# Two rows a partition of w_out fetched by two GpSimd gathers, and the z projection computed in rows

## The chip, the cores and the metric

The kernel runs on one core of one Trainium2 chip. The metric is the device time of one execution in microseconds (us). Before the change the median of three runs is 126.91 us (126.79 to 127.1). The profiled execution that all the rows below come from took 126.89 us; its span, from the first to the last instruction, is 125.1 us, so 1.8 us lie around it.

## The reference

One token `x` (1 x 576) is normalised and sent down two branches, which are added to it:

```python
xn = _layernorm(x, axis=-1)
return x + _A_ref(xn, k_cache, v_cache, wq, wo) + _B_ref(xn, w_in, w_sp, b_sp, w_out)

# A: attention of one token, 32 query heads on 16 key heads, the last 4096 positions
q = x @ wq                                   # 576 -> 32 heads x 128
scores = einsum('bhqd,bhkd->bhqk', q, k) * 128 ** -0.5
o = einsum('bhqk,bhkd->bhqd', softmax(scores), v)
A = o.reshape(1, 1, 4096) @ wo               # 4096 -> 576

# B: a gated MLP, sequence length 1
z = gelu(x @ w_in)                           # 576 -> 4608
z1, z2 = z[..., :2304], layernorm(z[..., 2304:])
B = (z1 * (w_sp * z2 + b_sp)) @ w_out        # 2304 -> 576
```

All inputs are bfloat16. Keys and values of the window are 16 MB each; with wq, wo, w_in and w_out some 51 MB are read once. There is one token, so every weight is used for one vector.

## The kernel before

The order of the instructions on every engine is written out by hand. All large loads are on one queue, SP's, in the order in which they are consumed: wq, the keys of head group 0 and 1 (four key heads a group, 4 MB each), w_in, keys 2, values 0, keys 3, values 1, 2 and 3, w_out, and wo in five pieces of 14, 9, 6, 2 and 1 rows a partition. They share four SBUF slots (`a` to `d`); a load is issued when the last reader of its slot is done. w_out and wo share two slots (`ends`).

Small vectors come first: x is normalised into `XT` (L206 to L209), the query is computed (L217) and spread into `Qb` (L245). Then come, for each group g and each half c of its positions:

- `keys(g, c)` (L258): VectorE (DVE) transposes the keys, four instructions of 128x1024.
- `scores(g, c)` (L265): TensorE (PE), 16 matmuls into the PSUM tile `S`.
- `sm_a(g)` (L286 to L292): the maximum of the scores on DVE, then four exponentials on ScalarE (ACT).
- `sm_b(g)` (L303, L306): DVE transposes the probabilities, ACT copies them into `PT`.
- `sums`, `pv(g)` (L329): 32 matmuls of the probabilities with the values into `ops`.
- `tail(g)` (L319 to L357): DVE scales and folds `ops`, PE moves it into place (L350), and DVE copies it into `Y`.

Branch B lies between them. `z_mms` (L365) takes x as the moving operand: 162 matmuls, each with 128x128 weights of w_in and two columns, so that z stands in columns (partition p holds 18 elements of each half). It comes on PE after the scores of groups 0 and 1. `z_exp` (L372 to L379) begins on DVE with one copy out of PSUM; it comes after `sm_b(1)` and before `keys(2, 1)`. `z_gelu` and `z_norm` follow later and leave `hv`, 18 columns, one for each row of w_out that a partition holds.

At the end PE adds everything into two accumulators, one for columns 0 to 263 and one for 264 to 575 of the output: `out_hv(0)` and `out_hv(1)` (12 rows of w_out) after `pv(3)`, then the matmuls of `tail(3)`, then `out_hv(2)` (six rows), then 32 rows of wo with `Y` (L465, two matmuls a row). DVE and ACT copy the accumulators out and ACT issues the store.

GpSimd (POOL) makes the identity and masks in the first 8 us, then has only two one-column powers to do (L200, L404).

Of the kernel before, what the change touches and what calls it, by code (L numbers as in the profile page):

```python
# [7 lines left out]

FP32 = mybir.dt.float32
BF16 = mybir.dt.bfloat16  # L10
ALU = mybir.AluOpType
ACT = mybir.ActivationFunctionType
AXX = mybir.AxisListType.X

D = 576
# [12 lines left out]
NF = FH // 128  # L28
CUT = (0, 264, D)
XP = D // 3  # L30
EPS = 1e-5
SCALE = DH ** -0.5
GELU_C = 0.7978845608028654
NS = 9


@with_exitstack
def kernel(
# [14 lines left out]
    nc = tc.nc  # L53
    P = nc.NUM_PARTITIONS
# [5 lines left out]
    work = ctx.enter_context(tc.tile_pool(name="work", bufs=2))  # L60
    ktpool = ctx.enter_context(tc.tile_pool(name="ktpool", bufs=2))
    single = ctx.enter_context(tc.tile_pool(name="single", bufs=1))
    ps_s = ctx.enter_context(tc.tile_pool(name="ps_s", bufs=1, space=bass.MemoryType.PSUM))
    ps_o = ctx.enter_context(tc.tile_pool(name="ps_o", bufs=1, space=bass.MemoryType.PSUM))
    ps_m = ctx.enter_context(tc.tile_pool(name="ps_m", bufs=1, space=bass.MemoryType.PSUM))
    ps_a = ctx.enter_context(tc.tile_pool(name="ps_a", bufs=1, space=bass.MemoryType.PSUM))
# [36 lines left out]
    V[2] = load_kv("b", A_v_cache, 2, "v")  # L103
    V[3] = load_kv("c", A_v_cache, 3, "v")
    ends = [big.tile([P, TP * DH], BF16, name=f"end{n}", tag="ad"[n]) for n in range(2)]
    wout_sb = rows(ends[0], B_w_out, "wout", 0, NF, 0)
    wo_sb = []
    for n, t, at in ((14, 1, 0), (9, 1, 14), (6, 0, NF), (2, 0, NF + 6), (1, 0, NF + 8)):
        wo_sb += rows(ends[t], A_wo, "wo", len(wo_sb), n, at * D)
# [64 lines left out]
    lx = const.tile([P, NG], FP32, name="lx")  # L174
    mb = const.tile([P, 32], FP32, name="mb")
    nc.gpsimd.memset(mb[:], 0.0)

# [32 lines left out]
    nc.tensor.matmul(ps_x[:, 24:26], lhsT=ones_b[:], rhs=spb[:], start=True, stop=True)  # L210
    wb = const.tile([P, 2], FP32, name="wb")
    nc.vector.tensor_copy(wb[:], ps_x[:, 24:26])


    for s, wv in wq_sb:
# [26 lines left out]
    for a in range(4):  # L242
        for h in range(2):
            for k2 in range(2):
                nc.vector.tensor_scalar_mul(qbv[:, a, h, k2], qpv[:, h, k2], mask4[:, a:a + 1])  # L245


    Y = const.tile([P, 32], BF16, name="Y")
    KT = {}
# [2 lines left out]
    def keys(g, c):  # L252

        kT = ktpool.tile([P, TC, 2, 8, GK, 2], BF16, name=f"kT{g}_{c}", tag="kT")
        src = K[g][:, TC * c:TC * (c + 1), :].rearrange("p t d -> p (t d)").bitcast(FP32)
        dst = kT[:].rearrange("p t b r x e -> p (t b r x e)").bitcast(FP32)
        for n in range(4):
            nc.vector.transpose(dst[:, 1024 * n:1024 * (n + 1)], src[:, 1024 * n:1024 * (n + 1)])  # L258
        KT[g, c] = kT

    def scores(g, c):
        kv = KT.pop((g, c))[:].rearrange("p (t s) b r x e -> p b e x t r s", s=2)
        for be in range(4):
            for x in range(GK):
                nc.tensor.matmul(  # L265
                    S[g % 2][32 * x:32 * x + 8, c, :],
                    lhsT=Qb[:, GK * g + x, be].rearrange("p a h -> p (a h)"),
                    rhs=kv[:, be // 2, be % 2, x],
                    start=(be == 0), stop=(be == 3), tile_position=(0, 32 * x),
                )  # L270
# [87 lines left out]


    def z_mms():  # L360
        zps = ps_a.tile([P, 2, NF], FP32, name="zps", tag="a")
        for s, wv in win_sb:
            wt = wv.rearrange("k (p t) -> k t p", t=NF)
            for t in range(NF):
                nc.tensor.matmul(zps[:, :, t], lhsT=wt[:, t, :], rhs=XT[:, s, :],  # L365
                                 start=(s == 0 and t == 0), stop=(s == NS - 1 and t == NF - 1),
                                 skip_group_check=True)
        return zps

    def z_exp(zps):  # L370
        z = const.tile([P, 2, NF], FP32, name="z")
        nc.vector.tensor_copy(z[:], zps[:])  # L372
        u = const.tile([P, 2, NF], FP32, name="u")
        nc.vector.tensor_mul(u[:], z[:], z[:])
        nc.vector.tensor_scalar(out=u[:], in0=u[:], scalar1=0.044715, scalar2=1.0,
                                op0=ALU.mult, op1=ALU.add)
        nc.vector.tensor_mul(u[:], u[:], z[:])
        th = const.tile([P, 2, NF], FP32, name="th")
        nc.scalar.activation(th[:], u[:], ACT.Exp, scale=-2.0 * GELU_C)  # L379
        return z, th  # L380
# [15 lines left out]
    def z_norm(G, sz):  # L396
        psz = ps_m.tile([P, 512], FP32, name="psz", tag="m")
        nc.tensor.matmul(psz[:, 0:2], lhsT=ones_f[:], rhs=sz[:], start=True, stop=True)
        mz = const.tile([P, 4], FP32, name="mz")
        nc.vector.tensor_scalar_mul(mz[:, 0:2], psz[:, 0:2], 1.0 / FH)  # L400
        nc.vector.tensor_mul(mz[:, 2:3], mz[:, 0:1], mz[:, 0:1])
        nc.vector.tensor_sub(mz[:, 2:3], mz[:, 1:2], mz[:, 2:3])
        nc.vector.tensor_scalar_add(mz[:, 2:3], mz[:, 2:3], EPS)  # L403
        nc.gpsimd.tensor_tensor(out=mz[:, 3:4], in0=mz[:, 2:3], in1=mhalf[:], op=ALU.pow)  # L404
        zn = const.tile([P, NF], FP32, name="zn")
        nc.vector.tensor_scalar(out=zn[:], in0=G[:, 1], scalar1=mz[:, 0:1], scalar2=mz[:, 3:4],
                                op0=ALU.subtract, op1=ALU.mult)
# [12 lines left out]
    for g in range(2):  # L420
        for c in range(2):
            keys(g, c)
            scores(g, c)
            if g == 1 and c == 0:
                sm_a(0)
# [27 lines left out]
    tail(1)  # L453
    sm_a(3)
    hv = z_norm(G, sz)
    sums(2)
    pv(2)
    tail(2)
    sm_b(3)
    sums(3)  # L460
    pv(3)

    def out_mms(lhs, col, wv, last):
        for n in range(2):
            nc.tensor.matmul(acc[n], lhsT=lhs[:, col:col + 1], rhs=wv[:, CUT[n]:CUT[n + 1]],  # L465
                             start=False, stop=last, tile_position=(0, 32 * n))
# [8 lines left out]
    out_hv(2)  # L475
    for t, wv in wo_sb:
        out_mms(Y, t, wv, t == 31)

    res = const.tile([1, D], BF16, name="res")
    nc.vector.tensor_copy(res[:, 0:CUT[1]], acc[0])  # L480
# [32 lines left out]
```

## Time and profile before

| | before |
|---|---|
| median of three runs | 126.91 us |
| profiled execution | 126.89 us |
| its span | 125.1 us |
| PE matmul busy | 70.8 us (57%), 626 instructions |
| DVE busy | 78.5 us (63%), 150 instructions |
| ACT busy | 43.2 us (34%) |
| POOL busy | 7.1 us (6%) |
| read from HBM | 50.96 MB, 407 GB/s over the span |
| mean granted PE clock | 0.754 |

Busy time alone names no bound here: no engine is over 63%, and the DMA engines move 407 GB/s over the span. The chain of work that ended last, the waits at the end, and the windows of the last microseconds have to be read together. In a row of the timeline the columns are: start, duration, engine, line, operation, result and operands, shape, count, and in brackets the idle time before it and what ended it. PEld is PE's weight load, which runs ahead of the matmuls.

### The profile page before, as it was taken

The page shows a single profiled execution, that of the slowest core. Times are in us where ns is not written, and L with a number is a line of the kernel's source. Part 1 is how long each engine was busy: PE and PEld are TensorE (multiplying, and loading weights), DVE is VectorE, ACT ScalarE, POOL GpSimd, SP SyncE. Part 2 cuts the span into 40 slices and gives each one's busy share as a digit, 9 for nine tenths or more (in the row PEclk, how much of TensorE's full clock was granted, in tenths as well). Part 3 has the DMA queues.
Part 4 walks back from the last instruction along what each step waited for, and adds up shares of the span by engine and source line. Part 5 has one row for each costly group of instructions (what it writes and reads, how often), then busy time and mean ns, then how long its engine had stood idle before and what let it go on. Part 6 is the DMA issues. An engine that isn't in the chain of part 4 may idle for free.

```text
span 125.1 us, 1617 instructions
## 1 busy us (share of the span) xinstructions
PE 70.8 (57%) x626; PEld 28.9 (23%) x626; DVE 78.5 (63%) x150; ACT 43.2 (34%) x101; POOL 7.1 (6%) x19
## 2 busy tenths in 40 slices
PE   0012841009878469998390992059892932049992
PEld 0001201001101013998000131002211411015850
DVE  6745025899799976308999367999938359003301
ACT  2100011000000956996069008707801941940001
POOL 2961000000000000000000000000000100000000
PEclk9999998555995867755559599657998555555899
DMA  4999899998999999898999989999999999999960
GB/s 118 511 422 440 385 471 440 398 492 356 487 420 402 385 493 461 377 492 372 461 451 398 482 367 477 401 451 430 409 482 398 451 394 440 418 413 416 428 237 0
DMA packets 2611, 51.06 MB, mean 408 GB/s; under 512 B 299, under 2 KB 428, under 8 KB 684
## 3 DMA queue, kind: packets, MB, share of 16 engines
q1 hardware_dynamic: 2592, 50.96, 95.2%
q8 instruction: 5, 0.08, 0.2%
q14 instruction: 2, 0.02, 0.0%
q10 hardware_dynamic: 12, 0.00, 0.0%
HBM read 50.96 MB, written 0.00 MB: 407 GB/s over the span
## 4 chain that ended last, share of the span: by engine, by line
DMA 61%; DVE 30%; PE 5%; SPq 1%; issue 1%; ACT 0%; DVEq 0%
DMA k<-in_A_k_cache_dram 37%; DMA end<-in_A_wo_dram 25%; DVE kT L258 22%; DVE pt L303 4%; PE S L265 3%; PE acc L465 1%; SPq L82 1%; DVE mx L286 1%; DVE on L343 1%; DVE om L339 1%; PE yps L350 0%; ACT res L481 0%; DVE rs L320 0%; DVE mt L275 0%; DVE mb L281 0%
## 5 line engine op out<-in xcount | busy, mean ns | idle before, releaser
L265 PE MATMUL S<-kT,Qb 128*8 128x512 bf16 x128 | 32.5, 1148 | 23.3 <-DVE kT L258 22.8
L258 DVE STREAM_TRANSPOSE kT<-k 128x1024 f32<-128x1024 f32 x32 | 36.8, 1207 | 6.5 <-DMA k<-in_A_k_cache_dram 6.5
L292 ACT ACTIVATE pz<-S,nm 32x1024 bf16<-32x1024 f32 x16 | 19.1, 1192 | 33.6 <-DVE nm L289 20.6
L306 ACT COPY PT<-pt 32x128 f32<-32x128 f32 x64 | 19.8, 309 | 17.2 <-DVE pt L303 16.5
L329 PE MATMUL ops<-v,PT 128*32 128x512 bf16 x128 | 11.0, 505 | 6.8 <-ACT PT L306 6.8
L265 PEld LDWEIGHTS <-Qb 128*8 128x8 bf16 x128 | 3.5, 96 | 45.0 <-issue 34.8
L303 DVE STREAM_TRANSPOSE pt<-pz 128x1024 f32<-128x1024 f32 x8 | 9.4, 1210 | 0.8 <-ACT pz L292 0.8
L339 DVE SCALAR_TENSOR_TENSOR om<-ops,rs,dmask 128x512 f32<-128x512 f32 x4 | 3.0, 750 | 10.5 <-PE ops L329 10.3
L365 PEld LDWEIGHTS <-win 128*128 128x128 bf16 x126 | 7.9, 165 | 1.9 <-issue 1.9
L365 PE MATMUL zps<-XT,win 128*128 128x2 bf16 x126 | 8.0, 202 | 0.0
L286 DVE TENSOR_REDUCE mx<-S 128x1 f32<-128x1024 f32 x4 | 4.9, 1214 | 3.9 <-PE S L265 3.9
L329 PEld LDWEIGHTS <-PT 128*32 128x32 bf16 x128 | 3.7, 117 | 11.5 <-ACT PT L306 6.9
L226 ACT CAST q_rep<-qps 128x512 bf16<-128x512 f32 x2 | 1.2, 586 | 14.9 <-DVE q_rep L228 14.9
L404 POOL TENSOR_TENSOR mz<-mz,mhalf 128x1 f32<-128x1 f32 x1 | 0.6, 554 | 85.5 <-DVE mz L403 85.5
L183 PE MATMUL ps_x<-ones_b,xtw 1*128 1x1 bf16 x9 | 0.4, 162 | 8.7 <-DVE xtw L181 8.7
L465 PE MATMUL acc<-end,Y 128*1 128x312 bf16 (+1 forms) x64 | 4.9, 285 | 0.3 <-DMA end<-in_A_wo_dram 0.3
L228 DVE CAST q_rep<-qps 128x512 bf16<-128x512 f32 x2 | 1.4, 692 | 5.1 <-PE qps L217 4.5
L481 ACT CAST res<-acc 1x312 bf16<-1x312 f32 x1 | 0.4, 411 | 11.7 <-PE acc L465 11.7
L350 PE MATMUL yps<-on,sel 128*32 128x32 f32 x32 | 2.0, 210 | 4.1 <-DVE on L343 4.1
L343 DVE TENSOR_REDUCE on<-om 128x128 f32<-128x512 f32 x4 | 4.2, 1042 | 0.1
L480 DVE CAST res<-acc 1x264 bf16<-1x264 f32 x1 | 0.4, 420 | 5.2 <-PE acc L465 5.2
L465 PE MATMUL acc<-end,hv 128*1 128x264 bf16 (+1 forms) x36 | 3.6, 360 | 0.0
(92 smaller groups left out, 56.6 us busy)
## 6 DMA issues: line engine op xcount, KB each, us to landing
k<-in_A_k_cache_dram SPq DMA_DIRECT2D x4, 4096.0 KB
v<-in_A_v_cache_dram SPq DMA_DIRECT2D x4, 4096.0 KB, 26.0
win<-in_B_w_in_dram SPq DMA_DIRECT2D x1, 4032.0 KB, 27.1
wq<-in_A_wq_dram SPq DMA_DIRECT2D x1, 3584.0 KB, 12.8
end<-in_B_w_out_dram SPq DMA_DIRECT2D x1, 2592.0 KB, 22.3
end<-in_A_wo_dram SPq DMA_DIRECT2D x1, 2016.0 KB
end<-in_A_wo_dram SPq DMA_DIRECT2D x1, 1296.0 KB
rest<-in_B_w_in_dram SPq DMA_DIRECT2D x1, 1152.0 KB
```

The lines of the kernel that those rows point to most:

```text
L258: nc.vector.transpose(dst[:, 1024 * n:1024 * (n + 1)], src[:, 1024 * n:1024 * (n + 1)])
L265: nc.tensor.matmul(S[g % 2][32 * x:32 * x + 8, c, :], lhsT=Qb[:, GK * g + x, be].rearrange("p a h -> p (a h)"), rhs=kv[:, be // 2, be % 2, x],
L286: nc.vector.tensor_reduce(out=mx[:, 0:1], in_=s[:], op=ALU.max, axis=mybir.AxisListType.XY)
L292: nc.scalar.activation(pz[lo:hi, :, :, x, :], s[lo:hi].rearrange("p a (t r e) -> p (a t) r e", r=8, e=2), ACT.Exp, bias=nm[lo:hi, 0:1], sc ...
L303: nc.vector.transpose(dst[:, 1024 * n:1024 * (n + 1)], src[:, 1024 * n:1024 * (n + 1)])
L306: nc.scalar.copy(PT4[32 * a:32 * a + 32, :, x, :], pt[32 * x:32 * x + 32, :, 2 * a:2 * a + 2])
L329: nc.tensor.matmul(ops[32 * q:32 * q + 32, :], lhsT=d["PT"][:, t0 // 2:t0 // 2 + 2].rearrange("p t x h e -> p (t x h e)"), rhs=V[g][:, t0: ...
L339: nc.vector.scalar_tensor_tensor(out=om[:].rearrange("p c d -> p (c d)"), in0=ops[:], scalar=d["rs"][:, 0:1], in1=dmask[:].rearrange("p c ...
L343: nc.vector.reduce_sum(on[:], om[:].rearrange("p c d -> p d c"), axis=AXX)
L350: nc.tensor.matmul(yps[32 * g:32 * g + 32, :], lhsT=sel[:, dq, :], rhs=d["on"][:, 32 * dq:32 * dq + 32], start=(dq == 0), stop=(dq == 3), ...
L365: nc.tensor.matmul(zps[:, :, t], lhsT=wt[:, t, :], rhs=XT[:, s, :], start=(s == 0 and t == 0), stop=(s == NS - 1 and t == NF - 1), skip_gr ...
L465: nc.tensor.matmul(acc[n], lhsT=lhs[:, col:col + 1], rhs=wv[:, CUT[n]:CUT[n + 1]], start=False, stop=last, tile_position=(0, 32 * n))
```

## The change

The last two of the 18 rows of w_out that each partition holds are no longer loaded on SP's queue. They go into a tile of their own, `ext`, by two gathers (indirect DMAs) that GpSimd issues. The first gather takes a partition's own two rows, but its table names a row out of range for 32 partitions (`SPARED`), and such rows are skipped. The second brings these 32 pairs of rows into 32 other partitions (`GIVEN`), and skips the remaining 96. `ext` is set to zero beforehand. The elements of `hv` that belong to the moved rows are moved to the same partitions by one matmul with a permutation (`move`, result `hx`).

The tables are made on GpSimd after L200 of before: each as a diagonal matrix, which PE turns into a column (`pick`) and DVE converts to integers (`idx`).

z is computed the other way round: x is the weight (32 columns, two of them used) and w_in is the moving operand, 288 columns at a time, in four column groups of PE; 72 matmuls instead of 162. The result stands in rows, in two PSUM tiles, and DVE turns it into the old layout with two 32x32-block transposes of 128x288 before the copy.

```diff
+NX = 2
+NM = NF - NX
+PAIRS = NF // NX
+FAR = 4096
+SPARED = ((20, 8), (52, 8), (68, 4), (88, 4), (100, 4), (120, 4))
+GIVEN = (72, 80, 104, 108, 112, 116)
+ZT = NF // 2
...
-    wout_sb = rows(ends[0], B_w_out, "wout", 0, NF, 0)
+    wout_sb = rows(ends[0], B_w_out, "wout", 0, NM, 0)
...
+    ext = far.tile([P, 2, NX, D], BF16, name="ext")
...
+    move = more.tile([P, P], BF16, name="move")
+    nc.vector.memset(move[:], 0.0)
+    XZ = more.tile([P, NS, 32], BF16, name="XZ")
+    nc.vector.memset(XZ[:], 0.0)
+    nc.vector.tensor_copy(XZ[:, :, 0:2], XT[:])
+    nc.vector.memset(ext[:], 0.0)
...
+    for (lo, n), at in zip(SPARED, GIVEN):
+        nc.gpsimd.tensor_copy(move[:, at:at + n], ident[:, lo:lo + n])
+    both = single.tile([P, 4, P], FP32, name="both", tag="pt")
+    which = []
+    for g in range(2):
+        col = both[:, 2 * g].bitcast(I32)
+        if g == 0:
+            nc.gpsimd.iota(col, pattern=[[PAIRS, P]], base=PAIRS - 1, channel_multiplier=0)
+            for lo, n in SPARED:
+                nc.gpsimd.memset(col[:, lo:lo + n], FAR)
+        else:
+            nc.gpsimd.memset(col, FAR)
+            for (lo, n), at in zip(SPARED, GIVEN):
+                nc.gpsimd.iota(col[:, at:at + n], pattern=[[PAIRS, n]], base=PAIRS * lo + PAIRS - 1, channel_multiplier=0)
+        diag = both[:, 2 * g + 1]
+        nc.gpsimd.tensor_copy(diag, col)
+        nc.gpsimd.tensor_tensor(out=diag, in0=diag, in1=ident[:], op=ALU.mult)
+        which.append(diag)
+
+    pick = ps_m.tile([P, 2], FP32, name="pick", tag="m")
+    for g, diag in enumerate(which):
+        nc.tensor.matmul(pick[:, g:g + 1], lhsT=diag, rhs=ones_f[:, 0:1], start=True, stop=True)
+
+    def rows_to_take():
+        idx = more.tile([P, 2], I32, name="idx")
+        nc.vector.tensor_copy(idx[:], pick[:])
+        which[:] = [idx[:, g:g + 1] for g in range(2)]
+
+    def load_ext():
+        pairs = B_w_out.rearrange("(r s) c -> r (s c)", s=NX)
+        for g in range(2):
+            nc.gpsimd.indirect_dma_start(
+                out=ext[:, g].rearrange("p s c -> p (s c)"), out_offset=None, in_=pairs,
+                in_offset=bass.IndirectOffsetOnAxis(ap=which[g], axis=0),
+                bounds_check=P * PAIRS - 1, oob_is_err=False)
...
     def z_mms():
-        zps = ps_a.tile([P, 2, NF], FP32, name="zps", tag="a")
+        zps = [pool.tile([P, ZT, 32], FP32, name=f"zps{n}", tag="ab"[n]) for n, pool in enumerate((ps_a, ps_b))]
         for s, wv in win_sb:
-            wt = wv.rearrange("k (p t) -> k t p", t=NF)
-            for t in range(NF):
-                nc.tensor.matmul(zps[:, :, t], lhsT=wt[:, t, :], rhs=XT[:, s, :],
-                                 start=(s == 0 and t == 0), stop=(s == NS - 1 and t == NF - 1),
-                                 skip_group_check=True)
+            wt = wv.rearrange("k (q p t) -> k q t p", q=4, t=NF)
+            for n in range(2):
+                for q in range(4):
+                    nc.tensor.matmul(zps[n][32 * q:32 * q + 32], lhsT=XZ[:, s, :], rhs=wt[:, q, ZT * n:ZT * (n + 1), :],
+                                     start=(s == 0), stop=(s == NS - 1), tile_position=(0, 32 * q))
...
-        nc.vector.tensor_copy(z[:], zps[:])
+        zt = q_rep[:].rearrange("p m b a d -> p (m b a d)").bitcast(FP32)[:, 0:32 * NF]
+        for n in range(2):
+            nc.vector.transpose(zt[:, 32 * ZT * n:32 * ZT * (n + 1)], zps[n][:].rearrange("p t c -> p (t c)"))
+        nc.vector.tensor_copy(z[:], zt.rearrange("p (t c) -> p t c", c=32)[:, :, 0:2].rearrange("p t h -> p h t"))
...
             keys(g, c)
+            if g == 0 and c == 0:
+                rows_to_take()
             scores(g, c)
...
     hv = z_norm(G, sz)
+    load_ext()
     sums(2)
     pv(2)
     tail(2)
     sm_b(3)
+    hx_ps = ps_m.tile([P, 32], FP32, name="hx_ps", tag="m")
+    nc.tensor.matmul(hx_ps[:, 0:NX], lhsT=move[:], rhs=hv[:, NM:NF], start=True, stop=True)
+    hx = more.tile([P, NX], BF16, name="hx")
+    nc.vector.tensor_copy(hx[:], hx_ps[:, 0:NX])
     sums(3)
     pv(3)
...
     for t, wv in wo_sb:
         out_mms(Y, t, wv, t == 31)
+        if t == 13:
+            for j in range(NX):
+                out_mms(hv, NM + j, ext[:, 0, j, :], False)
+                out_mms(hx, j, ext[:, 1, j, :], False)
```

More of the change, by code (lines that the diff above doesn't have):

```diff
@@ L10 @@
 BF16 = mybir.dt.bfloat16
+I32 = mybir.dt.int32
 ALU = mybir.AluOpType
@@ L62 @@
     single = ctx.enter_context(tc.tile_pool(name="single", bufs=1))
+    gap = ctx.enter_context(tc.tile_pool(name="gap", bufs=1))
+    far = ctx.enter_context(tc.tile_pool(name="far", bufs=1))
+    more = ctx.enter_context(tc.tile_pool(name="more", bufs=1))
     ps_s = ctx.enter_context(tc.tile_pool(name="ps_s", bufs=1, space=bass.MemoryType.PSUM))
@@ L176 @@
     nc.gpsimd.memset(mb[:], 0.0)
+    gap.tile([P, 176], BF16, name="unused")
+    ext = far.tile([P, 2, NX, D], BF16, name="ext")
     xtw = const.tile([1, NS, D // NS, 2], BF16, name="xtw")
```

## The prediction

> **What bounds the kernel now.** I read the end first, in the chain that ended last, then the timeline of the tail, then windows of it.
>
> The chain, in order of time (start, us, what):
>
> ```profile
> 32.81 23.86 DMA k<-in_A_k_cache_dram
> ...
> 56.69 4.62 DVE kT L258 x4
> 61.31 2.25 DVE pt L303 x2
> 63.56 0.09 DVE z L372
> ...
> 64.32 4.55 DVE kT L258 x4
> 68.87 0.04 issue
> 68.91 4.05 PE S L265 x16
> ...
> 90.41 30.86 DMA end<-in_A_wo_dram
> 121.27 0.04 issue
> 121.31 1.39 PE acc L465 x17
> ```
>
> Up to 56.69 a transfer decides; then DVE works without a pause, `z_exp` (L372 to L377) among it, and hands over to PE. The chain jumps to the last transfer at 90.41 only because that landing ends the last wait. How much the compute chain lacks of being last is in the tail's timeline:
>
> ```profile
> 111.04 3.60 PE L329 MATMUL ops<-v,PT 128*32 128x512 bf16 x32 [6.81 <-ACT PT L306]
> ...
> 117.30 0.20 DVE L357 CAST Y<-yps 32x32 bf16<-32x32 f32 x1 [0.78 <-PE yps L350]
> ...
> 117.66 3.03 PEld L465 LDWEIGHTS <-Y 128*1 128x1 bf16 x45
> ...
> 121.31 0.90 PEld L465 LDWEIGHTS <-Y 128*1 128x1 bf16 x16 [0.62 <-issue]
> 122.38 0.08 PEld L465 LDWEIGHTS <-Y 128*1 128x1 bf16 x1 [0.17 <-issue]
> ```
>
> From 117.55 on PE does the 64 matmuls of wo. It pauses only 0.62 us before the six-row piece and 0.17 before the last row: 0.79 us in all. Transfers and compute end almost together; a later compute chain has 0.79 us of cover, and beyond it the end moves one for one.
>
> The DMA share in windows of the end:
>
> ```profile
> 119.50:120.00 0.50, 0.50 (x13) 0.31 (x8) 0.00 (x0) 0.00 (x0) 0.00 (x0) 1.00 0.97 380
> 120.00:120.50 0.50, 0.50 (x10) 0.31 (x9) 0.00 (x0) 0.00 (x0) 0.00 (x0) 1.00 0.75 288
> 120.50:121.00 0.50, 0.50 (x5) 0.14 (x2) 0.00 (x0) 0.00 (x0) 0.00 (x0) 1.00 0.46 162
> 121.00:121.50 0.50, 0.22 (x5) 0.16 (x5) 0.00 (x0) 0.00 (x0) 0.00 (x0) 1.00 0.24 92
> 121.50:122.00 0.50, 0.50 (x12) 0.45 (x9) 0.00 (x0) 0.00 (x0) 0.00 (x0) 1.00 0.18 65
> ```
>
> The last but one number is the share of 16 engines: 0.24 is four engines, still at work when the rest is done. The trace's landing records agree: of the last row of wo ten engines land by 120.9, two by 121.3, four between 122.05 and 122.34. The four trail because of instruction packets:
>
> ```profile
> q8 instruction: 5, 0.08, 0.2%
> ```
>
> They start at 36.5, 57.2, 77.7, 101.0 and 120.6 and take 0.93 to 0.96 us. Before the first, the 16 engines land the keys of group 0 within 0.5 us of each other; after the fourth, four land 1.2 to 1.5 us behind the rest.
>
> **The change, part by part.** The sum is made against the profiled execution, 126.89 us; the median is 126.91, so 0.02 more.
>
> *The two rows off SP's queue.* Two rows are 2 x 1152 B in 8 partitions of an engine, 18.4 KB; at 408 GB/s over 16 engines (25.5 each) that is 0.72 us. If the four spared are the four that trail, they end at 122.34 - 0.72 = 121.6; the engines that take their share end at 120.9 + 0.72 = 121.6 as well. So the transfers may end 0.7 us earlier. By this alone the end could come up to 0.7 us earlier, if PE were ready.
>
> *The matmuls of these rows* change side. Four leave `out_hv(2)`, which ran while PE waited for Y (117.30 to 117.5): worth nothing. Eight enter after row 13 of wo, behind Y: 2 rows x 2 gathers x 2 accumulators. PE steps 3.03 / 45 = 0.067 us a matmul there: +0.54 us.
>
> *z on DVE* (L372): one copy of 0.16 us becomes two transposes of 128x288 and a copy of the same size. Rows: a transpose of 128x1024 takes 1.207 us, four take 4.62, so the step is (4.62 - 1.207) / 3 = 1.14; one of 128x32 takes 0.213. On the line between, 288 columns take 0.213 + 256 x 0.994 / 992 = 0.47, the step 0.40: two take 0.87 us. Bounds: 2 x 1.14 x 288 / 1024 = 0.64 if only columns cost, 2 x 1.207 = 2.4 if each took the long row's time; I take 0.87, as both neighbours are measured. This lies on the chain: DVE goes from `pt` through `z` to `kT` with no pause, PE starts `scores(2, 1)` when `kT` ends (68.91), and then `sm_a(2)`, `tail(0)`, `keys(3)`, `sm_a(3)`, `pv(2)`, `sm_b(3)` and `pv(3)` follow, each released by the step before it. The loads that these steps need land earlier than they start, so nothing absorbs the shift: Y comes 0.87 us later, at 118.4.
>
> *z on PE.* 72 matmuls of 288 columns are 20,736 columns. The scores' 16 x 512 columns, also strided, take 4.05 us, 2.0 columns a ns: 10.3 us. The query's 28 x 512 contiguous columns take 3.16 us, 4.5 a ns: 4.6 us. Before it took 7.97 + 2.37 = 10.3. It may last until DVE wants z at 63.5 (14.7 us from 48.8), and the keys of group 3, whose slot it frees at 59.06, queue behind values 0, which land at 66.3. So nothing either way.
>
> *Tables.* On DVE three memsets and a copy, of which `ext` is the long one (1,152 words; the 1,024 of S took 0.91 us), about 1.6 us, in its wait from 12.70 to 17.19. On POOL 26 small instructions behind L200 (11.66); its rows lie between 0.1 and 0.6 us, so 3 to 16 us; PE wants them only after `Qb` (23.2), and its first scores start at 28.33. If that cover goes, DVE still waits 5.44 us for the keys of group 2 at 56.69. `pick` costs about 0.6 us of a PE idle for 5; `idx` (0.16) is queued between the halves of group 0, ahead of DVE's 0.69 us wait at 33.47. `hx` stands in PE's idle stretch from 103.4 to 111.0, its copy in DVE's from 106.3 to 114.7. All nothing.
>
> *The gathers.* POOL issues them after L404, at about 98.6, on a queue of its own; SP's and ACT's queues are passed by none. SP's loads behind them keep their order; w_out's own has two rows less. `ext` is wanted at 118.4 + 28 x 0.067 = 120.3. If each row waits behind one SP packet of 0.6 to 1.2 us, 16 rows need 10 to 19 us: 108 to 118, in time. What a row costs its engine beyond its bytes no trace shows. Least: nothing. Most, by the instruction packets: one of 16 KB takes 0.95 us where SP's 16,128 B take 0.60, and stretches the SP packet beside it by 0.5; 0.85 us a packet. By bytes this is 0.12 a row, 1.9 us for 16 rows, and engines that take over rows would end at 123.5; per packet it is over 10. I take a small extra, below 1.4 us, which hides: PE now wants the last row at 123.0. A gather moves kilobytes as the loads do, and nothing else in it resembles an instruction store.
>
> In a sentence that the sum does not use: the Trainium skill (DMA: Bandwidth & Descriptors, "Issuing engines are not separate DMA queues") says that DMAs of all issuers share the same 16 engines and a second issuer saves only issue time, which speaks against a gain from the second queue itself; by it the transfers gain only what the uneven engines allow, the 0.7 above. No run here shows yet which engine a skipped row spares.
>
> **Sum.** +0.87 (z on DVE) + 0.54 (eight matmuls behind Y) - 0.79 (both waits of PE gone, as the landings come earlier and PE later) = +0.62: 127.5 us. PE, not the transfer, sets the end.
>
> **Rivals.**
>
> 1. *Faster: `pv(2)` gets the full clock.* Its 32 matmuls take 3.60 us at a granted 0.50, as `pv(3)` above, against 1.91 at 1.00 (`pv(0)`). The clock fell at 96.0 after a window in which PE was busy 1.68 of 3.41 us:
>
> ```profile
> 92.59:96.00 3.41, 1.68 (x14) 0.62 (x9) 1.94 (x5) 0.00 (x0) 0.00 (x0) 1.00 0.94 404
> 96.00:99.41 3.41, 2.75 (x26) 1.43 (x30) 1.92 (x12) 2.80 (x5) 0.55 (x1) 0.50 0.98 423
> ```
>
> The shift brings 0.87 us more of `scores(3, 1)` into it, 2.5 of 3.41. If that keeps the clock, `pv(2)` ends 1.2 to 1.7 us earlier, and DVE starts the last `pt` at 102.5 (end of the exponentials) instead of 104.4. Then the transfers set the end, 0.7 earlier: 126.2. [...] Chance 0.18. The Trainium skill (TensorE: Matmul & The Clock Gate, "What's actually happening") says that the window is free-running and doesn't start with the kernel; by it the shift would not win this each time, and the time stays 127.5 in most executions. The rows show only that the clock falls at multiples of 3.41 us.
>
> 2. *Slower by the gathers:* rows cost their engines more than 1.9 us, by the packet price above. At 0.3 us a row, 16 rows take 4.8; the engines end at 126.4, 3.4 us beyond what PE wants: 131. At 0.2 it is 129.3. Chance 0.12.
>
> 3. *No change: the chain has cover that I don't see*, and Y does not come later. Then 0.54 - 0.79 = -0.25: 126.6. For it: DVE idles 2.9 us before L286 and 1.9 before L339. Against it: both idle stretches end with PE work that begins only when the shifted step ends. Chance 0.18.
>
> 4. *The spared engines aren't those that trail*, as PE's stream loses 169 instructions and a packet may go elsewhere or fall away. The transfers then end at 122.3 to 123.1, PE is ready at 123.0: 127.5 to 127.6, the same number; it is inside my forecast, with 0.52 together.
>
> **How the numbers follow.** This kernel's runs differ by 0.3%, which is 0.38 us. My forecast's own range is 127.2 to 128.0 (0.64 to about 1.3 for the transposes). It counts 0.44 as slower, 0.08 as the same. Rival 1 is faster, rival 2 slower, rival 3 two thirds same, one third faster. Faster 0.24, same 0.20, slower 0.56. The range takes in rivals 1 and 3 and leaves out rival 2 and the far end of the transposes: 126.2 to 128.3.
>
> **What would show it.** Right: two transposes of about 0.45 us between the second `pt` and `kT` at 63.5; `Y` at about 118.4; 72 weight loads behind it without a pause; a DMA share that ends by 121.6; z on PE 5 to 11 us. Wrong: a pause of PE at `ext` or at the last rows; the engines' shares at the end no more even; Y at 117.5 or earlier; a granted clock of 1.0 at 98.

## The result, and the profile after

The changed kernel takes 127.94 us (median of 22 runs, 126.52 to 128.25); the kernel before takes 126.91 (22 runs beside them, 126.79 to 127.42). The ratio is 1.0069, with a 95% interval from 1.0053 to 1.0086: slower by 0.9 us by the ratio, by 1.0 by the medians. The profiled execution took 127.82 us, its span is 125.8, so 2.0 us lie around it where 1.8 lay before. Nearly all runs lie between 127.5 and 128.25, but two are at 126.52 and 126.72; what tells the two kinds apart is a question of its own below.

The chain that ended last, in order of time (start, us, what):

```profile
63.60 0.74 DVE q_rep L429 x2
64.34 0.02 issue
64.36 0.20 DVE z L430
...
65.23 4.54 DVE kT L313 x4
69.78 0.04 issue
69.82 4.03 PE S L320 x15
...
92.15 29.68 DMA end<-in_A_wo_dram
121.83 0.04 issue
121.87 1.47 PE acc L530 x18
```

The two transposes stand where they were forecast, and `scores(2, 1)` starts at 69.82 instead of 68.91: +0.91. But the chain still jumps to the last transfer, and that ends 0.56 us later than before (121.87 against 121.31), not earlier. The timeline of the tail:

```profile
111.03 3.60 PE L384 MATMUL ops<-v,PT 128*32 128x512 bf16 x32 [4.22 <-ACT PT L361]
...
117.27 0.20 DVE L412 CAST Y<-yps 32x32 bf16<-32x32 f32 x1 [0.76 <-PE yps L405]
...
117.52 1.76 PE L530 MATMUL acc<-end,Y 128*1 128x264 bf16 x26
...
119.81 1.46 PE L530 MATMUL acc<-end,Y 128*1 128x264 bf16 x18
...
121.87 1.45 PE L530 MATMUL acc<-end,Y 128*1 128x264 bf16 x18 [0.60 <-DMA end<-in_A_wo_dram]
121.87 0.97 PEld L530 LDWEIGHTS <-Y 128*1 128x1 bf16 x16 [0.94 <-issue]
123.02 0.08 PEld L530 LDWEIGHTS <-Y 128*1 128x1 bf16 x1 [0.18 <-issue]
```

Two things differ from the forecast. `Y` (117.27) is no later than before (117.30). And both pauses are still there, though PE has eight matmuls more ahead of them. Read in the weight loads, as in the prediction, they are 0.94 us before the six-row piece, where it was 0.62, and 0.18 before the last row. (The row of the matmuls shows only 0.60 for the first, as that row ends at 121.27 and the row of the loads at 120.9.) The DMA share in windows of the end (the last number but one):

```profile
120.50:121.00 0.50, 0.50 (x11) 0.34 (x7) 0.00 (x0) 0.00 (x0) 0.00 (x0) 1.00 0.53 198
121.00:121.50 0.50, 0.27 (x3) 0.00 (x0) 0.00 (x0) 0.00 (x0) 0.00 (x0) 1.00 0.20 74
121.50:122.00 0.50, 0.13 (x3) 0.10 (x4) 0.00 (x0) 0.00 (x0) 0.00 (x0) 1.00 0.07 28
122.00:122.50 0.50, 0.50 (x11) 0.49 (x9) 0.00 (x0) 0.00 (x0) 0.00 (x0) 1.00 0.06 21
```

Before, four engines were still at work (0.24, 0.18). Now the share falls to 0.06, which is one engine of 16, and that one works on until 122.7. The landing records of the last row of wo, one per engine, in order:

```
before   120.43 120.46 120.52 120.54 120.56 120.65 120.66 120.67 120.81 120.86 121.17 121.28 122.04 122.07 122.17 122.34
changed  120.24 120.38 120.67 120.72 120.73 120.76 120.85 120.94 121.34 121.41 121.42 121.46 121.48 121.61 121.76 122.98
```

Fifteen engines do what was forecast, an end by 121.6, within 0.2 us. One lands at 122.98, and PE waits for it. The records of single packets say which one it is. The DMA queues of the page:

```profile
q0 software_dynamic: 160, 0.30, 0.6%
q8 instruction: 4, 0.07, 0.2%
```

PE's instructions now come in four 16 KB packets, not five, at 37.7, 65.7, 94.6 and 119.8 us. Followed from packet to packet (on one engine the next packet starts within some 15 ns of the end of the one before), the last three fall on engines whose rows are spared. The first falls on an engine that takes over rows: it carries 16 row pairs and the packet, and is the one at 122.98. So the spared engines are mostly the late ones, but not all the late ones are spared.

Why `Y` is not late, although the chain was shifted by 0.91 us at 69.82 and by 1.26 at the `Y` of group 1 (95.19 against 93.93), is seen at `pv(2)`. Its row before the change, from the timeline:

```profile
97.14 3.60 PE L329 MATMUL ops<-v,PT 128*32 128x512 bf16 x32
```

and after it:

```profile
98.21 2.53 PE L384 MATMUL ops<-v,PT 128*32 128x512 bf16 x32
```

with these windows after the change (the number after the five engines is the granted clock of PE, 1.00 and 0.99):

```profile
92.59:96.00 3.41, 2.94 (x22) 0.88 (x14) 1.24 (x3) 0.00 (x0) 0.00 (x0) 1.00 0.98 418
96.00:99.41 3.41, 1.49 (x26) 0.95 (x30) 2.42 (x12) 1.55 (x3) 0.66 (x2) 0.99 0.89 384
```

The clock of the second window is 0.99 where it was 0.50. In the window ahead PE was busy for 2.94 of 3.41 us with the shift, where it had been 1.68. `pv(2)` gains 1.07 us, and DVE starts the last `pt` at 103.55 as before.

The parts of the change that were to be hidden are hidden. z on PE and DVE:

```profile
49.30 7.46 PE L421 MATMUL zps<-win,XZ 128*32 128x288 bf16 x56
...
56.53 2.29 PE L421 MATMUL zps<-rest,XZ 128*32 128x288 bf16 x16
...
63.52 0.80 DVE L429 STREAM_TRANSPOSE q_rep<-zps 128x288 f32<-128x288 f32 x2
```

The tables and the gathers:

```profile
23.54 0.98 PE L288 MATMUL pick<-ones_f,both 128*128 128x1 f32 x4 [2.92 <-DVE Qb L264]
28.36 0.13 DVE L292 CAST idx<-pick 128x2 int32<-128x2 f32 x1
...
99.32 1.26 POOL L298 DMA_INDIRECT ext<-in_B_w_out_dram,idx  x1 [0.32 <-issue]
...
100.89 1.00 POOL L298 DMA_INDIRECT ext<-in_B_w_out_dram,idx  x1 [0.30 <-issue]
```

The tables take POOL from 12.97 to 16.80 and delay nobody: the keys of group 2 land at 56.70 (56.69 before) and DVE goes on at once. The gathers land by 108.4 and 111.9; the first matmul that needs them runs at 119.1.

### The profile page after: what moved, and what is told of

Read it like the earlier page. It is cut to its first block, busy times and chain, and to the rows that moved or that the text cites. A ratio compares the mean times of both kernels' runs of the same rounds, so it can differ in the third digit from the quotient of the medians.

```text
span 125.8 us, 1494 instructions
## 1 busy us (share of the span) xinstructions
PE 71.2 (57%) x545; PEld 23.1 (18%) x545; DVE 81.0 (64%) x158; ACT 43.4 (34%) x101; POOL 12.7 (10%) x45
## 4 chain that ended last, share of the span: by engine, by line
DMA 60%; DVE 23%; PE 13%; SPq 2%; issue 1%; ACT 0%
DMA k<-in_A_k_cache_dram 36%; DMA end<-in_A_wo_dram 24%; DVE kT L313 18%; PE S L320 6%; PE ops L384 3%; DVE pt L358 2%; SPq L93 2%; PE acc L530 1%; DVE on L398 1%; PE lps L367 1%; DVE om L394 1%; DVE q_rep L429 1%; PE yps L405 0%; ACT res L550 0%; PE acc L499 0%
## 5 line engine op out<-in xcount | busy, mean ns | idle before, releaser
L421 PE MATMUL zps<-win,XZ 128*32 128x288 bf16 x56 | 7.5, 697 | 0.0
L530 PE MATMUL acc<-end,Y 128*1 128x264 bf16 (+1 forms) x64 | 4.9, 285 | 0.6 <-DMA end<-in_A_wo_dram 0.6
L367 PE MATMUL lps<-lx,lsum 128*128 128x1 f32 x8 | 2.1, 329 | 4.6 <-DVE hx L524 2.5
L421 PEld LDWEIGHTS <-XZ 128*32 128x32 bf16 x72 | 2.8, 117 | 7.4 <-issue 7.4
L530 PEld LDWEIGHTS <-Y 128*1 128x1 bf16 x64 | 3.4, 83 | 1.8 <-issue 1.1
```

The costliest lines, as they stand in the source:

```text
L421: nc.tensor.matmul(zps[n][32 * q:32 * q + 32], lhsT=XZ[:, s, :], rhs=wt[:, q, ZT * n:ZT * (n + 1), :], start=(s == 0), stop=(s == NS - 1), ...
```

## The experiments

Two explanations stand against each other in them. The transfers' one, theory A of the expectations: an instruction packet of PE on an engine that also takes over rows makes one landing late, and that sets the end. PE's one, theory B or P, is the prediction's own: later `Y` and eight matmuls more behind it set the end. Medians of one group share the runs of the kernel before.

### First group: the parts apart (before: 126.81 us, 17 runs)

**Rows counted by engine.** The tables are replaced, so that engine e gets e row pairs and part of w_out is left out: the trace then tells by a packet count which engine is which. The diffs here are against the changed kernel.

```diff
+        have = []
+        for e in range(16):
+            own = [64 * (e >> 3) + 4 * (e & 7) + 32 * h + i for h in range(2) for i in range(4)]
+            have += own[:min(8, e)] if g == 0 else own[:max(0, e - 8)]
```

> The changed kernel, but the two gathers bring engine e exactly e row pairs (e from 0 to 15, engines by partitions as the change takes them: 8 for each half of the partitions, four partitions each in turn), and nothing else of the last two rows of w_out; so part of w_out is left out, and each engine can be told by the bytes that GpSimd's queue gave it. Theory A (the end was set by one engine that takes over rows and also fetched instructions): the first instruction packet, at about 37 us, falls on an engine with 10 to 13 pairs, the next three on engines with 5, 6, 9 or 14. Theory B (the recorded sum: PE sets the end): which engine fetches doesn't matter. A third way: the packets fall on other engines in each load, and no engine can be named.

Measured: 127.86. Of the four instruction packets the first, at 37.6, is on the engine with 13 pairs, that is engine 13, which in the changed kernel takes rows over; those at 65.6 and 94.7 are on engines 14 and 5, both spared there; the fourth (120.3) can't be assigned. The last landing is at 122.63, but PE does not wait for it: `Y` comes at 118.01 here, and PE runs through. So where the packets fall is confirmed, while this execution's end is PE's.

**z in rows alone**, without gathers.

```diff
-    wout_sb = rows(ends[0], B_w_out, "wout", 0, NM, 0)
+    wout_sb = rows(ends[0], B_w_out, "wout", 0, NF, 0)
...
-    load_ext()
```

> The kernel before with z in rows alone; w_out on SP's queue as before, no gathers. Theory A: four engines carry instruction packets and three trail by some 1.4 us at the end, as four did before, so the transfers end as before, at about 122.3; 126.9 us, within 0.3%. Theory B: DVE +0.87, of which 0.79 are covered by PE's waits: 127.0. If z alone were what costs, it would be 127.6 or more.

Measured: 126.88 (12 runs, 126.61 to 127.66), ratio 1.0012 (0.9998 to 1.0025). From the timeline of its profile (126.61):

```profile
97.95 1.91 PE L333 MATMUL ops<-v,PT 128*32 128x512 bf16 x32
...
116.05 0.20 DVE L361 CAST Y<-yps 32x32 bf16<-32x32 f32 x1 [0.53 <-PE yps L354]
...
121.02 1.36 PE L472 MATMUL acc<-end,Y 128*1 128x264 bf16 x18 [0.71 <-DMA end<-in_A_wo_dram]
```

The transposes alone cost nothing that can be measured in the median. In this execution, the fastest of the twelve, the clock does not fall ahead of `pv(2)` at all (1.91 us), `Y` comes at 116.05, and the transfers set the end, at 122.05.

**The gathers alone**, z in columns as before.

```diff
-        zps = [pool.tile([P, ZT, 32], FP32, name=f"zps{n}", tag="ab"[n]) for n, pool in enumerate((ps_a, ps_b))]
+        zps = ps_a.tile([P, 2, NF], FP32, name="zps", tag="a")
...
-            nc.vector.transpose(zt[:, 32 * ZT * n:32 * ZT * (n + 1)], zps[n][:].rearrange("p t c -> p (t c)"))
-        nc.vector.tensor_copy(z[:], zt.rearrange("p (t c) -> p t c", c=32)[:, :, 0:2].rearrange("p t h -> p h t"))
+        nc.vector.tensor_copy(z[:], zps[:])
```

> The changed kernel with z in columns as before; the gathers stay. Theory A: five instruction packets; if the first falls on an engine that takes over rows, that engine lands at about 123 and the time is 127.8 as with z in rows. Theory B: eight matmuls +0.54, waits -0.79: 126.6.

Measured: 127.75, ratio 1.0073 (1.006 to 1.0086); the six times are 126.74, 127.65, 127.72, 127.79, 127.83 and 128.06. The profile is the one of 126.74. From its timeline:

```profile
119.68 2.58 PE L524 MATMUL acc<-end,Y 128*1 128x264 bf16 x33
```

A window of its end (the DMA share, last but one, is 0.00):

```profile
121.50:122.00 0.50, 0.50 (x9) 0.28 (x5) 0.00 (x0) 0.00 (x0) 0.00 (x0) 1.00 0.00 0
```

Here the forecast came true: the first four of the five packets all fall on spared engines, the fifth (121.1) on one that has finished, all landings lie between 120.46 and 121.61, and PE runs through. So the lists of spared engines fit the stream with z in columns. That the same kernel mostly takes 1 us longer shows that something else goes wrong in it most of the time.

**The takers moved** to four other engines, z in rows.

```diff
-GIVEN = (72, 80, 104, 108, 112, 116)
+GIVEN = (0, 8, 32, 36, 40, 44)
```

> The changed kernel with the moved rows given to the first four engines (partitions 0 to 15 and 32 to 47) in place of 10 to 13. Theory A: the engine with the first packet now has its own two rows only, and ends 0.7 us earlier: about 127.1, if the first four fetch no instructions. Theory B: nothing changes, 127.9.

Measured: 127.48 (six runs, 127.26 to 127.89), ratio 1.0057 (1.0042 to 1.0072). Two weight loads of the profile (127.26):

```profile
121.32 0.97 PEld L530 LDWEIGHTS <-Y 128*1 128x1 bf16 x16 [0.26 <-issue]
...
122.46 0.08 PEld L530 LDWEIGHTS <-Y 128*1 128x1 bf16 x1 [0.17 <-issue]
```

The packet at 36.6 now falls on an engine with its own eight pairs. Its last landing comes at 122.42, eight pairs less than 122.98, and it is still the last: the last weight load waits for it and starts at 122.46. From the first profile of the changed kernel to this one the last landing comes 0.56 us earlier, and so does the end (127.82 to 127.26). In the medians the gain is not clear of the noise, as the intervals of the two ratios overlap.

### Second group: one term at a time (before: 126.97 us, 17 runs)

**The gathers alone, once more**, the same kernel as above, to see one of its long executions.

> Gathers alone, z in columns, a second look: the first profile was of an execution at 126.74, and five others took 127.65 to 128.06. Theory P (PE: the eight matmuls behind Y use up the cover, and Y comes between 117.3 and 118.3 as the clock falls): at about 127.8 the profile shows Y near 118.2 and no pause of PE behind it. Theory A (an engine that takes over rows and fetched instructions lands last): Y near 117.3, a pause of PE of 0.6 us or more before the last 18 matmuls, and one engine alone in the last half us.

Measured: 128.11. The timeline of its tail:

```profile
116.36 0.20 DVE L409 CAST Y<-yps 32x32 bf16<-32x32 f32 x1 [0.67 <-PE yps L402]
...
120.83 1.23 PE L524 MATMUL acc<-end,Y 128*1 128x264 bf16 x16 [0.47 <-DMA end<-in_A_wo_dram]
123.31 0.30 PE L524 MATMUL acc<-end,Y 128*1 128x264 bf16 x2 [1.25 <-DMA end<-in_A_wo_dram]
```

`Y` is nearly a microsecond early, and PE stands still for 1.25 us before the very last row. The fifth packet, at 121.3, fell on an engine that was still at work; it lands at 123.27, the other fifteen by 121.84. Before the change the last packet cost nothing as its engine had finished.

**Without the eight matmuls** behind `Y`.

```diff
             for j in range(NX):
-                out_mms(hv, NM + j, ext[:, 0, j, :], False)
-                out_mms(hx, j, ext[:, 1, j, :], False)
+                pass
```

> The changed kernel without the eight matmuls with ext; the last two rows of w_out are loaded and left out of the sum. Theory P: 0.54 us less behind Y, 127.94 becomes 127.4. Theory A: the transfers set the end as before, 127.9.

Measured: 127.89 (six runs, 127.19 to 128.01), ratio 1.0055 (1.0035 to 1.0076): the same as the changed kernel. The timeline (127.98):

```profile
117.62 0.20 DVE L412 CAST Y<-yps 32x32 bf16<-32x32 f32 x1 [0.53 <-PE yps L405]
117.87 3.45 PE L530 MATMUL acc<-end,Y 128*1 128x264 bf16 x46
122.02 1.46 PE L530 MATMUL acc<-end,Y 128*1 128x264 bf16 x18 [0.70 <-DMA end<-in_A_wo_dram]
```

PE is done earlier and waits longer, for an engine with 16 pairs and the packet of 36.7, whose landing is alone at 123.14. The eight matmuls are real work, but they are not what costs in the median.

**Without the gathers' transfer**: tables, `move` and the eight matmuls stay, the rows are never fetched.

```diff
-        for g in range(2):
+        for g in range(0):
             nc.gpsimd.indirect_dma_start(
```

> The changed kernel without its two gathers; ext stays zero, so the last two rows of w_out count for nothing, and 0.3 MB less are read. All matmuls stay. Theory P: 127.9 still, in most executions. Theory A: no engine has more than its share, all land 0.7 us earlier than before the change: 126.9 or less.

Measured: 127.10 (12 runs, 126.79 to 127.87), ratio 1.002 (1.0001 to 1.0039). In the profile (126.82) the last landing is at 121.57, `Y` at 117.18, and PE runs through. Without the rows the engine with the packet is no later than 121.6, and most of the loss is gone, although `Y` and the eight matmuls are as in the changed kernel. It does not reach the kernel before.

**The changed kernel once more**, unaltered.

> The changed kernel once more, for a second profile. Theory A: the last engine is again alone in the last half us, and it carries the packet of 37 us and eight packets of the gathers. Theory P: the first profile was of the rarer kind, and this one has Y near 118.2 and no pause of PE.

Measured: 127.87. The timeline of its tail:

```profile
117.99 0.20 DVE L412 CAST Y<-yps 32x32 bf16<-32x32 f32 x1 [0.53 <-PE yps L405]
...
120.61 2.77 PE L530 MATMUL acc<-end,Y 128*1 128x264 bf16 x33
...
121.94 0.97 PEld L530 LDWEIGHTS <-Y 128*1 128x1 bf16 x16 [0.29 <-issue]
...
123.08 0.08 PEld L530 LDWEIGHTS <-Y 128*1 128x1 bf16 x1 [0.17 <-issue]
```

And the window in which `pv(2)` begins, with the granted clock of PE behind the engines:

```profile
96.00:99.41 3.41, 1.81 (x18) 1.04 (x22) 2.38 (x13) 1.88 (x3) 0.98 (x2) 0.55 0.91 394
```

The transfers are as in the first profile: the packet of 37.8 on an engine with 16 pairs, its landing alone at 123.04, the rest by 121.72. But now the clock fell early (0.55 in the window), `pv(2)` took 3.60 us, and `Y` comes at 117.99. The merged row of 33 matmuls hides it, but the weight loads still wait, 0.29 us before the six-row piece and 0.17 before the last row, which starts at 123.08, behind the landing at 123.04. So the transfers set the end of this execution too, with `Y` 0.7 us later than in the first.

### Third group: the engines chosen anew (before: 126.84 us, 27 runs)

**Spared and taking engines chosen for z in rows**: spared are those on which the packets were seen in the first group, and no taker gets one.

```diff
-SPARED = ((20, 8), (52, 8), (68, 4), (88, 4), (100, 4), (120, 4))
-GIVEN = (72, 80, 104, 108, 112, 116)
+SPARED = ((20, 8), (52, 8), (68, 4), (100, 4), (84, 8), (116, 8))
+GIVEN = (72, 104, 0, 96, 28, 60)
```

> The changed kernel with other lists: the engines that fetch in this program (by the counted rows 13, 14 and 5, and 6 or 9) spared, five in all, and their rows given to 0, 7, 8, 10 and 11. Theory A: no engine both takes over rows and fetches; the last landing falls from 123.0 to about 121.7, and the time to that of the kernel without the transfers, 127.1 with the same spread, 126.8 to 127.9, which is then PE's. If it stays at 127.9, the packet of 37 us is not what made the last engine last.

Measured: 127.69, ratio 1.0052 (1.0027 to 1.0078). The ten times fall into 126.67, 126.87, 127.01, 127.05 and 127.66 to 128.25. The profile is one of 127.05; from its timeline:

```profile
117.39 0.20 DVE L412 CAST Y<-yps 32x32 bf16<-32x32 f32 x1 [0.53 <-PE yps L405]
...
120.00 2.58 PE L530 MATMUL acc<-end,Y 128*1 128x264 bf16 x33
```

The window that was at a DMA share of 0.07 in the changed kernel:

```profile
121.50:122.00 0.50, 0.50 (x11) 0.33 (x7) 0.00 (x0) 0.00 (x0) 0.00 (x0) 1.00 0.00 0
```

All four packets now stand on engines without rows, all landings come by 121.79, and PE runs through. In this execution the transfers' part of the loss is gone. But the expected 127.1 is missed: the times spread, the median is only a quarter of a microsecond below that of the changed kernel, and the intervals of the two ratios overlap.

**The same, for z in columns**, with takers away from the fifth packet.

```diff
-GIVEN = (72, 80, 104, 108, 112, 116)
+GIVEN = (28, 60, 0, 8, 96, 40)
...
-            nc.vector.transpose(zt[:, 32 * ZT * n:32 * ZT * (n + 1)], zps[n][:].rearrange("p t c -> p (t c)"))
+        nc.vector.tensor_copy(z[:], zps[:])
```

> The gathers with z in columns, the rows given to engines 0, 2, 7 and 8. Here five packets are fetched, the fifth at 121.2. Theory A: that packet now falls on an engine that is done by then; the last landing is 121.6 in every execution, and the time 126.7 in most, where it was 127.75. If it stays near 127.8, the fifth packet follows the takers.

Measured: 127.05 (11 runs, 126.94 to 127.49), ratio 1.0019 (1.001 to 1.0027), against 1.0073 for the gathers alone with the first takers. Moving rows from four engines to four others is worth 0.7 us, as the transfers' explanation has it. The expected 126.7 is missed. The last landing in the profile is 122.26, not 121.6, and the packet records show why: the fifth packet came at 119.8 here, not at 121.2, on an engine with its own eight pairs that was still at work. That engine lands last, the other fifteen by 121.81.

**And the eight matmuls ahead of those with `Y`**, directly behind `out_hv(2)`; the diff is against the kernel just told of.

```diff
     out_hv(2)
+    for j in range(NX):
+        out_mms(hv, NM + j, ext[:, 0, j, :], False)
+        out_mms(hx, j, ext[:, 1, j, :], False)
```

> As the one before, and the eight matmuls with ext put ahead of Y's, behind the last rows of w_out. With the landings out of the way PE sets the end, so some 0.25 of the 0.54 us can go: 126.5, 0.3% below the kernel before. If the landings still set the end, the same as the one before.

Measured: 127.09 (12 runs, 126.4 to 127.7), ratio 1.0023 (1.0007 to 1.0039). Two of the twelve, 126.40 and 126.44, are the shortest times of any kernel here; the timeline of the one of 126.44:

```profile
115.91 0.20 DVE L409 CAST Y<-yps 32x32 bf16<-32x32 f32 x1 [0.53 <-PE yps L402]
...
120.61 1.36 PE L524 MATMUL acc<-end,Y 128*1 128x264 bf16 x18 [0.73 <-DMA end<-in_A_wo_dram]
```

All landings come by 121.60 and set the end: this is what the gathers could bring. The median is not below the kernel before, so the expectation is missed, and the cause in the other ten was not seen.

**The engines chosen for z in rows, once more**, the same kernel as the first of this group (beside it one run of the kernel before, 126.94).

> The kernel with the spared and taking engines chosen for z in rows, once more, to see one of its slow executions from inside: its ten times lay between 126.67 and 127.05 (four) and between 127.66 and 128.25 (six), and the execution seen so far, 127.05, had Y at 117.39, all landings by 121.79 and no pause of PE. Theory: with the landings even only PE's chain is left, and it moves with the clock that pv(2) gets. By it an execution above 127.6 has Y at 117.9 or later, the last landing still by 121.9, and PE does its last 33 matmuls without a pause. Rival: the instruction packets stand elsewhere in the slow executions, one of them on an engine that takes rows over. By it an execution above 127.6 has one engine's last landing at 122.6 or later, alone, and PE pauses 0.5 us or more ahead of the last pieces, with Y at 117.4 or earlier. An execution of 127.1 or less says nothing on either, apart from repeating the even landings.

Measured: 126.78, one of the short ones. From its timeline:

```profile
98.06 2.66 PE L384 MATMUL ops<-v,PT 128*32 128x512 bf16 x32
...
117.12 0.20 DVE L412 CAST Y<-yps 32x32 bf16<-32x32 f32 x1 [0.62 <-PE yps L405]
```

The window of `pv(2)`'s begin, at a granted clock of 0.95 where the second execution of the changed kernel had 0.55:

```profile
96.00:99.41 3.41, 1.63 (x26) 1.02 (x30) 2.42 (x12) 1.71 (x3) 0.80 (x2) 0.95 0.89 384
```

The even landings repeat (all by 121.72), and the packets stand on the same kinds of engines as in the first execution. A long execution of this kernel was not caught, so what sets its end is not shown.

### All profiles with the tables and z in rows, side by side

The moment at which the clock falls is worked out from the mean granted clock of 1 us windows (0.68 in the window from 99 means 0.36 us at 1.0, the rest at 0.5). The waits are those of the weight loads of wo, between `Y` and the last row.

| kernel | clock falls | `pv(2)` us | `Y` | last landing | weight loads wait | time |
|---|---|---|---|---|---|---|
| changed | 99.4 | 2.53 | 117.27 | 122.98 | 0.94 + 0.18 | 127.82 |
| changed, again | 96.4 | 3.60 | 117.99 | 123.04 | 0.29 + 0.17 | 127.87 |
| rows counted | 96.5 | 3.61 | 118.01 | 122.63 | none | 127.86 |
| no eight matmuls | 97.9 | 3.44 | 117.62 | 123.14 | 0.42 + 1.04 + 0.18 | 127.98 |
| takers moved | 99.5 | 2.52 | 117.40 | 122.42 | 0.26 + 0.17 | 127.26 |
| no transfer | 98.7 | 2.91 | 117.18 | 121.57 | none | 126.82 |
| engines chosen | 98.4 | 3.30 | 117.39 | 121.79 | none | 127.05 |
| engines chosen, again | 99.1 | 2.66 | 117.12 | 121.72 | none | 126.78 |

Two limits can be read off. Where the last weight load waits for the last landing, the time is that landing + 4.84 us within 0.01 (the four rows with waits above; in the gathers alone 123.27 and 128.11; in the eight matmuls ahead 121.60 and 126.44). One profile has more, 122.26 and 127.49, with 2.4 us around its span; the kernels without the tables have less, 4.55 and 4.56 us (before the change 122.34 and 126.89, z in rows alone 122.05 and 126.61). Where PE runs through, the time is `Y` + 9.64 to 9.67 us (the gathers alone among them, 117.07 and 126.74), and 9.85 where 2.2 us lie around the span (the rows counted).

Both profiles of the changed kernel stand at the transfers' limit: 122.98 and 123.04 give 127.82 and 127.88. PE's limit is close behind in the second: a `Y` at 117.99 gives 127.65. So the late landing costs the loss seen in both, but with even landings a late `Y` would still cost most of it. To be back near 126.8 both must be away.

## Why the prediction was right in its number, and where its working failed

The number 127.5 was 0.4 us low, and the time lies in its range; the forecast of a loss held. But three of its own signs of being wrong came: a pause of PE at the last rows, `Y` in use from 117.52 instead of 118.4, and a granted clock of 0.99 around 98. The sum of the profiled execution, term by term, from 126.89 to 127.82:

| step | predicted | measured |
|---|---|---|
| `Y` later (z on DVE) | +0.87 | -0.03 (117.30 to 117.27) |
| PE's work from `Y` to the six-row piece (eight matmuls) | +0.54 | +0.27 (4.01 - 0.62 to 4.60 - 0.94) |
| PE's waits, in the weight loads | -0.79 | +0.33 (0.79 to 1.12) |
| the rest, to the end of the span | 0 | +0.13 (rounded spans) |
| around the span | 0 | +0.23 (1.79 to 2.02) |
| sum | +0.62 | +0.93 |

That the sums come near each other is luck: `Y` falls short of its term by 0.90 us, the waits exceed theirs by 1.12.

**z on DVE.** The size was right: two transposes in 0.80 us (0.87 predicted), and `scores(2, 1)` 0.91 later. That it arrives at `Y` in full is wrong. `Y` lay at 117.1 to 118.0 in eight profiles, so between -0.2 and +0.7, and at 116.05 with z in rows alone. In the table it goes with the moment at which the clock falls. Rival 1 had this mechanism, with the right sign: where the clock falls at 98.7 or later, `pv(2)` gives back 0.7 to 1.1 us, less than the 1.2 to 1.7 forecast. Its time, 126.2, did not come, as the landings were not early. The Trainium skill (TensorE: Matmul & The Clock Gate, "What's actually happening") calls the window free-running, so that the transition varies from one execution to the next; the trace agrees: in one program with the same shift it fell at 96.4 and at 99.4. How busy PE was in the 3.41 us ahead does not settle it alone: after 2.25 us (92.96 to 96.37, the changed kernel's second profile) the clock fell, after 2.05 (96.31 to 99.72, z in rows alone) it stayed at 1.0 until 103.1. The prediction's "in most executions" was too firm: three of the eight profiles have `pv(2)` above 3.4 us.

**Eight matmuls behind `Y`**: +0.54 predicted, and the whole stretch is 0.27 longer. The prediction took the four that left `out_hv(2)` as worth nothing; before the change a weight load for `hv` still stood at 117.56, behind the first for `Y`, so they were probably not free. Taking the eight out changes nothing in the median (127.89), since PE then waits longer.

**The waits of PE** are the step that failed: "both waits of PE gone, as the landings come earlier", and with it "PE, not the transfer, sets the end". Fifteen engines landed by 121.76 (forecast 121.6) and one later than any before, at 122.98 against 122.34, so the waits grew to 1.12 us and the transfer set the end. The reason is rival 4, which the prediction priced at 122.3 to 123.1 and put inside its forecast: the stream of PE lost enough instructions (162 in the trace, 169 in the prediction) for one packet to fall away, and the first packet moved to an engine that takes rows over. Its upper end, 122.34 + 0.72, is an engine late by both, its packet and its eight extra pairs, and that is what came. What the prediction lacked is that this alone, without PE being late, gives the same time: it let PE be ready only at 123.0. That the engines matter is shown in both directions: the gathers without z in rows had even landings where the fifth packet came to an engine that had finished (126.74) and a landing at 123.27 where it came to a taker still at work (128.11); with lists chosen for z in rows the landings were even in both profiles.

The Trainium skill (Runtime: NRT & Kernel Launch, "Instruction fetch mechanics") says that instructions are fetched in blocks of 16 KB, 256 instructions each, and that a block's cost is mostly hidden. The trace agrees on the blocks: five became four as PE went from 626 to 545 matmuls, each with a weight load. No wait of PE is put down to a block here, but the DMA engine that carries it is late by about 1.4 us, and in the end the kernel pays.

**What the gathers cost their engines.** Rival 2 is excluded. In the first profile the engine without packet and pairs lands at 120.24, those with 16 pairs and no packet at 121.4 to 121.8: 1.2 to 1.5 us for 16 pairs, 0.07 to 0.10 each. The bytes alone, 2304 at 25.5 bytes a ns, give 0.09.

**Hidden parts.** The tables (3.8 us on POOL, 0.98 on PE, 0.13 on DVE), `move`, `hx` and the gathers' issue are hidden, as predicted. z on PE took 7.46 + 2.29 = 9.75 us (4.6 to 10.3 predicted); the scores' row was the right one to take.

**Rival 3**, no change, did not come for the whole, but z in rows alone behaves that way (126.88 against 126.81).

**Not foreseen**: about 0.2 us more around the span. The profiles of kernels with the tables have 1.9 to 2.0 us there (two have 2.2 and 2.4), also without the gathers' transfer; z in rows alone and the kernel before have 1.8. What of the tables' edits costs it was not tried.

**What stays open.** Why two runs of the changed kernel came at 126.5 and 126.7. What sets the end in the long executions with the engines chosen anew: the four between 127.66 and 127.76 fit a `Y` that moves with the clock (118.0 gives 127.65), but no such execution was seen, and 127.99 and 128.25 lie above that. What moves the fifth packet with z in columns: it came at 119.8, 120.4, 121.1 and 121.3 in four profiles, and cost time in the first and the last. What decides which engine carries an instruction packet: in profiles of one program the packets up to 101 us stood on the same kinds of engine, from one program to another they moved.

## What to carry to other kernels

Where the load is spread by hand over uneven DMA engines, the unevenness has a cause, and the same edit can move it: a change in the number of PE's instructions can move the instruction packets to other engines. So count the packets of the changed program before choosing which engines to relieve, and look at the last landing of each engine, not at the mean share. And when two limits lie within a few tenths of each other, a sum along one chain can give the right number with the wrong terms; test it by removing a term, and see whether the time moves. Look for waits in the weight loads too: a merged row of matmuls can hide them.

## What the runs showed of the hardware

- One 16 KB instruction packet delays its DMA engine by about 1.4 us: 0.88 to 0.97 us of its own, and the load's packet behind it is stretched, from 1.19 to 1.66 us or from 1.21 to as much as 1.83. The delay stays with the engine to the end of the queue: the first packet, at 37.7 us, still shows in the landing at 122.98. Without the gathers' rows the three engines with a packet up to 94.7 us land at 121.46 to 121.57, the others by 120.80.
- The entries of a gather that are skipped still make packets: 64 of 8 bytes (9 ns each) for 128 skipped entries. The rows that are fetched went in packets of 4608 bytes, two pairs, at 0.178 us each, and an engine took one of these and one of SP's in turn.
- The granted clock of PE fell at 96.4 to 99.5 us in the eight profiles of the table, whose instructions stood at nearly the same places, and with z in rows alone only at 103.1; `pv(2)`, 32 matmuls of 512 columns, took 1.91 us where the clock stayed at 1.0 and 3.60 where it was 0.5.
